# Moving the first weight slice, two early loads and two groups' attention steps in a fused attention and FFN kernel

## The chip, the cores and the metric

The kernel runs on one core of one Trainium2 chip. The metric is the device time of one execution in microseconds (us). Times are shown beside a profile of a single execution, whose span runs from the first to the last instruction on the core.

The names used below: PE is TensorE (matmuls), PEld its weight loads, ACT is ScalarE, DVE is VectorE, POOL is GpSimd. SP is SyncE, which here only issues DMAs; its queue is worked off in order, so an entry that waits holds back those behind it.

## The reference

Attention in chunks of 64 tokens, then an FFN with a squared ReLU over all tokens:

```python
# q, k, v: (8, 8, 576, 64) float32; w_in: (512, 2048); w_out: (2048, 512)
scores = scale * np.matmul(q_c, k_c.transpose(0, 1, 2, 4, 3))   # within each chunk of 64
attn = np.exp(scores - max) ; attn = attn / sum
out = np.matmul(attn, v_c)                                      # (B, H, S, D)
x = out.transpose(0, 2, 1, 3).reshape(B * S, H * D)             # 4608 tokens x 512
h = np.maximum(x @ w_in, 0.0)
y = h * h @ w_out                                               # 4608 x 512
```

## The kernel before

**Tiling.** The 4608 tokens are cut into 18 groups of 256 (GT), and the groups into nine blocks of two: block 0 is groups 0 and 1, block 1 is 3 and 2 (in that order), then 4 and 5, 6 and 7, and so on. So block 3 is groups 6 and 7. In each block PE does the FFN of its 512 tokens, and between these matmuls the attention of the next block's groups, so that PE always has FFN matmuls to do while other engines work on the attention.

**Steps of a group.** Loads of q, k and v (`qk_pieces`, `v_pieces`: lists of DMAs on SP; v goes in separate pieces of even and odd heads, L117 and L124). Transposed q and k, called qkT: groups 0 to 3 on PE (`transpose_qk`, L164 and L173; TE, TA and TM differ in the PSUM banks), the others by a cast to bf16 on POOL (C, `cast_qk`, L212) and a DMA transpose on SP (TD, L219). Scores (SC, `scores`, L233 on PE, then Exp on ACT, L240). Values (AV, `values`, L257 on PE, two tiles; then a reciprocal and a product on DVE, L264 and L265, which give x). Transposed x, called xT (XT): groups 0 and 1 on PE a tile at a time (`transpose_x_early`, L195, L200), groups 2 to 5 on PE (L284), from group 6 on by a DMA transpose on SP (L278). xT of both groups is the moving operand of the block's FFN-in.

**FFN.** FFN-in (`ffn_in`, L316) has 16 steps of four matmuls over the block's columns, one step for each 128 of the 2048 hidden features; each ends in a Relu on ACT (L322) and a square on DVE (L323). FFN-out (`ffn_out`, L332) has four row tiles of 16 matmuls each, with a yield after every fourth; the result is copied on ACT (L349) and stored by POOL (L350). Block 0 uses `ffn_out_by_ft` (L361), which takes the w_out slices in order of arrival: 12 yields over the hidden features for all four tiles, then four, one for each tile.

**What sets the order.** Nothing reorders the instructions of an engine. Each `yield` of the FFN ends a slot; at a slot the loop at the end issues one load from `loads` (if the slot is in `go_slots`) and then the steps that `at(slot, step, group)` put down for it. In blocks 2 and later slots 0 to 15 are FFN-in and 16 to 31 FFN-out. The loads run one or two blocks ahead.

**Buffers and queues.** Weights come as 16 slices of 512 KB in float32 (eight of w_in by `load_w_in`, eight of w_out by `load_w_out`) through five staging buffers (`w_st`), and are cast to bf16 on POOL (L139, L147). So the sixth slice waits on SP for the cast of the first, and so on. In addition SP's DMAs use eight completion semaphores in turn: an entry waits for the one eight before it. `keep_busy(n)` issues n matmuls of the identity whose result nobody reads.

**The start.** SP loads q, k, v of groups 0 and 1. PE works through their attention with `keep_busy` in between. The first slice of w_in is issued from ACT's queue, in two casts; the other seven follow on SP behind the values of group 1. The generator `early` does FFN-in of the first two hidden steps in two halves, first for the 256 columns of group 0, then for group 1; two of these half steps are run before the last transpose of x. Then come eight w_out slices, then the loads of group 3 and of group 2.

Of the kernel before, what the change touches and what calls it, by code (L numbers as in the profile page):

```python
# [17 lines left out]
def kernel(  # L18
# [9 lines left out]
    nc = tc.nc  # L28
# [8 lines left out]
    n_ft = d_ff // 128  # L37
# [3 lines left out]
    blocks = [[0, 1], [3, 2]] + [[g, g + 1] for g in range(4, n_grp, 2)]  # L41
# [87 lines left out]
    def go(pieces):  # L129
        for f in pieces:  # L130
            f()

    def load_w_in(i, eng=nc.sync, n_cast=1):
        cols = slice(i * 256, (i + 1) * 256)
        st = wst_pool.tile([128, 1024], FP32, name="w_st").rearrange("p (a f) -> p a f", a=n_dt)
        eng.dma_start(out=st, in_=moe_w_in[:, cols].rearrange("(a p) f -> p a f", p=128))
        n = 256 // n_cast
        for c in range(0, 256, n):
            nc.gpsimd.tensor_copy(  # L139
                out=w_in_bf[:, :, i * 256 + c:i * 256 + c + n], in_=st[:, :, c:c + n])  # L140

    def load_w_out(i):
        st = wst_pool.tile([128, 1024], FP32, name="w_st").rearrange("p (a f) -> p a f", a=2)
        nc.sync.dma_start(
            out=st,
            in_=moe_w_out[i * 256:(i + 1) * 256, :].rearrange("(a p) f -> p a f", p=128))
        nc.gpsimd.tensor_copy(out=w_out_bf[:, 2 * i:2 * i + 2, :], in_=st)  # L147
# [40 lines left out]
    def transpose_x_early(g, t):  # L188
        j, c = place[g]
        if j not in xTs:  # L190
            xTs[j] = att_pool.tile([128, BT // 128, n_dt, 128], BF16, name="xT", bufs=2)
        psb = ps_ffn.tile([128, 512], FP32, name="ps_ffn").bitcast(BF16)
        x = state["x", g]
        for hp in range(n_hp):
            nc.tensor.transpose(  # L195
                out=psb[:, hp * 128:(hp + 1) * 128],
                in_=x[:, t, hp].rearrange("p a d -> p (a d)"),
                identity=ident)
        copy = nc.vector.tensor_copy if t else nc.scalar.copy
        copy(  # L200
            out=xTs[j][:, c // 128 + t].rearrange("p h q -> p (h q)"), in_=psb[:, 0:512])

    def keep_busy(n):
        ps = ps_ffn.tile([128, 512], FP32, name="ps_ffn")
        for _ in range(n):
            nc.tensor.matmul(out=ps[:, 0:128], lhsT=ident, rhs=ident, start=True, stop=True)  # L206
# [84 lines left out]
    C, TD = cast_qk, transpose_qk_dma  # L291
    SC, AV, XT = scores, values, transpose_x
# [4 lines left out]
    def TE(g):  # L297
        transpose_qk(g, ps_ffn, ps_ffn)
# [10 lines left out]
    def ffn_in(j, parts):  # L309
        if j not in gTs:  # L310
            gTs[j] = ffn_pool.tile([128, n_ft, BT], BF16, name="gT")
        gT, xT = gTs[j], xTs[j]
        for c, n, ft in ((c, n, ft) for c, n, fts in parts for ft in fts):
            h = ps_ffn.tile([128, 512], FP32, name="ps_ffn")
            for dt in range(n_dt):
                nc.tensor.matmul(  # L316
                    out=h[:, 0:n],
                    lhsT=w_in_bf[:, dt, ft * 128:(ft + 1) * 128],
                    rhs=xT[:, c // 128:(c + n) // 128, dt, :],
                    start=(dt == 0), stop=(dt == n_dt - 1))  # L320
            rl = ffn_pool.tile([128, 512], BF16, name="rl", bufs=3)
            nc.scalar.activation(out=rl[:, 0:n], in_=h[:, 0:n], func=AF.Relu)  # L322
            nc.vector.tensor_tensor(  # L323
                out=gT[:, ft, c:c + n], in0=rl[:, 0:n], in1=rl[:, 0:n], op=ALU.mult)
            yield
# [28 lines left out]
    def ffn_out_by_ft(j):  # L354

        gT = gTs.pop(j)
        n_tt = len(blocks[j]) * GT // 128
        o_ps = [ps_ffn.tile([128, d_model], FP32, name="ps_ffn") for _ in range(n_tt)]

        def mm(tt, ft):  # L360
            nc.tensor.matmul(  # L361
                out=o_ps[tt],
                lhsT=gT[:, ft, tt * 128:(tt + 1) * 128],
                rhs=w_out_bf[:, ft, :],
                start=(ft == 0), stop=(ft == n_ft - 1))

        for ft in range(n_ft - 4):
            for tt in range(n_tt):
                mm(tt, ft)
            yield  # L370
        for tt in range(n_tt):
            for ft in range(n_ft - 4, n_ft):
                mm(tt, ft)
            o_sb = ffn_pool.tile([128, d_model], FP32, name="o_sb", bufs=4)
            nc.scalar.copy(out=o_sb, in_=o_ps[tt])
            t0 = blocks[j][tt // 2] * GT + tt % 2 * 128
            nc.gpsimd.dma_start(out=out[t0:t0 + 128, :], in_=o_sb)
            yield

    def pieces(grps):  # L380
        for g in grps:
            yield from qk_pieces(g)
        for g in grps:
            yield from v_pieces(g)

    go(pieces([0, 1]))
    TE(0)
    keep_busy(8)
    SC(0)
    keep_busy(6)  # L390
    TE(1)
    load_w_in(0, nc.scalar, 2)
    keep_busy(8)
    SC(1)
    keep_busy(10)
# [5 lines left out]
    keep_busy(10)  # L401
    transpose_x_early(0, 1)
    AV(1, [0])
    keep_busy(14)
    transpose_x_early(1, 0)
    keep_busy(8)
    AV(1, [1])
    n_early = 2
    early = ffn_in(0, [(0, 256, range(n_early)), (256, 256, range(n_early)),
                       (0, 512, range(n_early, n_ft))])  # L410
    next(early)
    next(early)
    transpose_x_early(1, 1)

    for i in range(1, 8):
        load_w_in(i)
    for i in range(8):
        load_w_out(i)
    for g in blocks[1]:
        go(pieces([g]))  # L420

    for j, grps in enumerate(blocks):
        nxt = blocks[j + 1] if j + 1 < len(blocks) else []
        far = blocks[j + 2] if j + 2 < len(blocks) else []
        plan = {}

        def at(slot, f, g):
            plan.setdefault(slot, []).append((f, g))

        if j == 0:  # L430
            loads, go_slots = pieces(far), range(17)
            for slot, f in ((24, TA), (27, SC), (29, AV), (31, XT)):
                at(slot, f, nxt[0])
            at(31, TM, nxt[1])
            phases = [early, ffn_out_by_ft(0)]
        elif j == 1:
            loads, go_slots = itertools.chain(*map(qk_pieces, far)), range(30, 48)
            for slot, f in ((3, SC), (6, AV), (11, XT)):
                at(slot, f, grps[1])
            for i, g in enumerate(nxt):  # L440
                for slot, f in ((16 + 4 * i, C), (21 + 4 * i, TD), (37, SC), (39 + 2 * i, AV),
                                (42 + 2 * i, XT)):
                    at(slot, f, g)
            for i, g in enumerate(far):
                at(36 + 4 * i, C, g)
                at(42 + 3 * i, TD, g)
            phases = [ffn_in(1, [(0, 256, range(n_ft)), (256, 256, range(n_ft))]), ffn_out(1)]
        else:
            loads, go_slots = pieces(far), range(32)
            slots = {SC: 9 if j == 3 else 8, AV: 11, XT: 15, C: 14, TD: 19}  # L450
            if j == 2:
                loads = itertools.chain(*map(v_pieces, nxt), loads)
                slots = {SC: 6, AV: 11, XT: 14, C: 20, TD: 24}
            for i, g in enumerate(nxt):
                at(slots[SC], SC, g)
                at(slots[AV] + 4 * i, AV, g)
                at(slots[XT] + 3 * i, XT, g)
            for i, g in enumerate(far):
                at(slots[C] + 2 * i, C, g)
                at(slots[TD] + 3 * i, TD, g)  # L460
            phases = [ffn_in(j, [(0, BT, range(n_ft))]), ffn_out(j)]
        slot = 0
        for phase in phases:
            for _ in phase:
                if slot in go_slots:
                    for f in loads:
                        f()
                        break
                for f, g in plan.get(slot, []):
                    f(g)  # L470
                slot += 1
        go(loads)
# [30 lines left out]
```

## Time and profile before

| | us |
|---|---|
| five runs | 301.45, 298.99, 296.71, 299.39, 298.08 |
| median | 298.99 |
| the profiled execution | 301.45 |
| its span | 299.7 |
| mean granted PE clock in it | 0.992 |
| FFN-in starts without a break (first L316 run) | 21.88 |
| FFN-out of block 0 starts (first L361) | 34.85 |
| block 2: FFN-in starts | 86.73 |
| block 2: FFN-out starts | 107.36 |
| block 3: FFN-in starts | 121.18 |
| last block: last L332 ends | 295.8 |

The profiled execution is the slowest of the five, so a sum over its parts is a sum against 301.45 and not against the median. From 121 us on each block takes 29.4 us (121.18, 150.71, 180.08, 209.44, 238.81 are the starts of FFN-in), and PE is busy almost throughout.

Where PE waits is read in its timeline from the bracket behind a row: idle time before the instruction, and what ended it. Where DMAs are late, the time to landing of a tile's DMAs says how long after its issue a transfer was complete. Some of them, issue and landing (us from the span's start):

| DMA | issued | landed |
|---|---|---|
| w_in, first slice (ACT's queue) | 12.09 | 18.55 |
| w_in, second slice (first one on SP) | 12.41 | 20.0 |
| w_out, last slice | 34.15 | 40.2 |
| k of group 3 | 35.08 | 43.85 |
| k of group 2, second part | 45.14 | 52.2 |
| qkT of group 5 | 71.41 | 75.63 |
| qkT of group 7 | 88.61 | 96.48 |
| xT of group 6 | 106.00 | 110.2 |
| qkT of group 9 | 121.00 | 127.7 |

### The profile page before, as it was taken

The page shows a single profiled execution, that of the slowest core. Times are in us where ns is not written, and L with a number is a line of the kernel's source. Part 1 is how long each engine was busy: PE and PEld are TensorE (multiplying, and loading weights), DVE is VectorE, ACT ScalarE, POOL GpSimd, SP SyncE. Part 2 cuts the span into 40 slices and gives each one's busy share as a digit, 9 for nine tenths or more (in the row PEclk, how much of TensorE's full clock was granted, in tenths as well). Part 3 has the DMA queues.
Part 4 walks back from the last instruction along what each step waited for, and adds up shares of the span by engine and source line. Part 5 has one row for each costly group of instructions (what it writes and reads, how often), then busy time and mean ns, then how long its engine had stood idle before and what let it go on. Part 6 is the DMA issues. An engine that isn't in the chain of part 4 may idle for free.

```text
span 299.7 us, 6440 instructions
## 1 busy us (share of the span) xinstructions
PE 282.2 (94%) x2608; PEld 142.8 (48%) x2628; DVE 114.4 (38%) x248; ACT 131.4 (44%) x228; POOL 67.6 (23%) x103
## 2 busy tenths in 40 slices
PE   2989999999895999999999999999999999999994
PEld 2764445885442444444444444444444444444441
DVE  1267812782422350355037405630562046205300
ACT  1526505773335531572167216711671177126511
POOL 2047832050070006023105013301320100020010
PEclk9999999999999799999999999999999999999999
DMA  7999999999999999998999899689987501310011
GB/s 206 240 346 364 331 290 218 292 198 209 209 219 175 227 195 230 241 220 170 254 243 222 168 267 248 112 165 276 241 133 152 161 35 24 83 72 35 0 70 70
DMA packets 156140, 57.03 MB, mean 190 GB/s; under 512 B 139280, under 2 KB 151824, under 8 KB 156112
## 3 DMA queue, kind: packets, MB, share of 16 engines
q1 hardware_dynamic: 152640, 46.81, 75.8%
q0 software_dynamic: 2800, 9.18, 9.2%
q10 hardware_dynamic: 672, 0.66, 0.7%
q8 instruction: 20, 0.33, 0.5%
q14 instruction: 8, 0.07, 0.1%
HBM read 36.70 MB, written 9.44 MB: 154 GB/s over the span
## 4 chain that ended last, share of the span: by engine, by line
PE 76%; DMA 17%; POOL 1%; issue 1%; DVE 1%; SPq 1%; ACT 1%; POOLq 0%; ACTq 0%
PE ps_ffn L316 34%; PE ps_ffn L332 33%; DMA k_sb<-in_k_dram 5%; DMA w_st<-in_moe_w_in_dram 4%; DMA qkT<-qkb 4%; PE ps_att L257 2%; PE ps_ffn L361 2%; DMA w_st<-in_moe_w_out_dram 2%; PE ps_att L233 2%; DMA q_sb<-in_q_dram 2%; DVE gT L323 1%; PE ps_ffn L164 1%; SPq L219 1%; POOL w_in_bf L139 1%; PE ps_ffn L206 1%
## 5 line engine op out<-in xcount | busy, mean ns | idle before, releaser
L316 PE MATMUL ps_ffn<-xT,w_in_bf 128*128 128x512 bf16 (+1 forms) x648 | 130.9, 359 | 1.3 <-DVE xT L200 1.1
L323 DVE TENSOR_TENSOR gT<-rl 128x512 bf16<-128x512 bf16 (+1 forms) x162 | 77.3, 493 | 131.8 <-ACT rl L322 129.7
L332 PE MATMUL ps_ffn<-w_out_bf,gT 128*128 128x512 bf16 x495 | 111.5, 379 | 1.1 <-issue 0.3
L322 ACT ACTIVATE rl<-ps_ffn 128x512 bf16<-128x512 f32 (+1 forms) x162 | 86.7, 553 | 39.8 <-PE ps_ffn L316 36.2
L316 PEld LDWEIGHTS <-w_in_bf 128*128 128x128 bf16 x648 | 62.3, 98 | 62.0 <-issue 2.8
L332 PEld LDWEIGHTS <-gT 128*128 128x128 bf16 x512 | 49.3, 98 | 58.0
L349 ACT COPY o_sb<-ps_ffn 128x512 f32<-128x512 f32 x31 | 18.2, 586 | 91.9 <-PE ps_ffn L332 91.9
L350 POOL DMA_DIRECT2D out_dram<-o_sb x31 | 16.8, 542 | 144.1 <-ACT o_sb L349 144.1
L212 POOL CAST qkb<-q_sb 128x1024 bf16<-128x1024 f32 x14 | 14.8, 1057 | 48.3 <-DMA q_sb<-in_q_dram 46.1
L265 DVE TENSOR_TENSOR x<-ps_att,rec 128x512 bf16<-128x512 f32 x36 | 24.9, 692 | 1.2
L240 ACT ACTIVATE e<-ps_att 128x1024 bf16<-128x1024 f32 x18 | 17.9, 1023 | 7.7 <-PE ps_att L233 7.7
L212 POOL CAST qkb<-k_sb 128x1024 bf16<-128x1024 f32 x14 | 15.4, 1098 | 2.1 <-DMA k_sb<-in_k_dram 2.0
L361 PE MATMUL ps_ffn<-w_out_bf,gT 128*128 128x512 bf16 x61 | 14.3, 379 | 0.3 <-issue 0.2
L264 DVE RECIPROCAL rec<-ps_att 128x8 f32<-128x8 f32 x36 | 7.2, 200 | 16.9 <-PE ps_att L257 16.9
L139 POOL CAST w_in_bf<-w_st 128x1024 bf16<-128x1024 f32 (+1 forms) x9 | 8.8, 981 | 19.1 <-DMA w_st<-in_moe_w_in_dram 19.1
L233 PE MATMUL ps_att<-qkT 64*64 64x64 bf16 x576 | 7.7, 197 | 4.6 <-DMA qkT<-qkb 4.2
L233 PEld LDWEIGHTS <-qkT 64*64 64x64 bf16 x576 | 6.0, 110 | 9.0 <-DMA qkT<-qkb 4.4
L257 PEld LDWEIGHTS <-e 64*64 64x64 bf16 x576 | 6.4, 107 | 7.0 <-DVE gT L323 2.5
L361 PEld LDWEIGHTS <-gT 128*128 128x128 bf16 x64 | 6.0, 98 | 7.2 <-issue 0.3
L147 POOL CAST w_out_bf<-w_st 128x1024 bf16<-128x1024 f32 x8 | 8.9, 1110 | 2.3 <-DMA w_st<-in_moe_w_out_dram 2.0
L257 PE MATMUL ps_att<-ve_sb,e 64*64 64x65 bf16 x288 | 8.6, 196 | 0.0
L257 PE MATMUL ps_att<-vo_sb,e 64*64 64x65 bf16 x288 | 8.6, 196 | 0.0
(34 smaller groups left out, 53.5 us busy)
## 6 DMA issues: line engine op xcount, KB each, us to landing
out_dram<-o_sb POOLq DMA_DIRECT2D x35, 256.0 KB, 4.1
q_sb<-in_q_dram SPq DMA_DIRECT2D x25, 256.0 KB, 5.2
k_sb<-in_k_dram SPq DMA_DIRECT2D x25, 256.0 KB, 4.9
ve_sb<-in_v_dram SPq DMA_DIRECT2D x32, 128.0 KB, 4.1
vo_sb<-in_v_dram SPq DMA_DIRECT2D x32, 128.0 KB, 3.9
w_st<-in_moe_w_out_dram SPq DMA_DIRECT2D x8, 512.0 KB, 5.8
w_st<-in_moe_w_in_dram SPq DMA_DIRECT2D x7, 512.0 KB, 7.1
q_sb<-in_q_dram SPq DMA_DIRECT2D x3, 512.0 KB, 6.7
```

Source lines behind the costliest of these rows:

```text
L212: nc.gpsimd.tensor_copy(out=qkb[:, which], in_=qk[g][which].rearrange("p t h d -> p (t h d)"))
L233: nc.tensor.matmul(out=ps[64 * c:64 * c + 64, o0:o0 + 64], lhsT=qkT[64 * a:64 * a + 64, 1, t, hp, cols], rhs=qkT[64 * a:64 * a + 64, 0, t, ...
L240: nc.scalar.activation(out=e.rearrange("p a h t q -> p (a h t q)"), in_=ps, func=AF.Exp, scale=scale)
L257: nc.tensor.matmul(out=ps[64 * p:64 * p + 64, a, hp * (D + 1):(hp + 1) * (D + 1)], lhsT=e[64 * c:64 * c + 64, a, hp, t, :], rhs=vb[64 * c: ...
L265: nc.vector.tensor_tensor(out=x[:, t].rearrange("p h a d -> p a h d"), in0=o[:, :, :, 0:D], in1=rec.to_broadcast([128, 2, n_hp, D]), op=AL ...
L316: nc.tensor.matmul(out=h[:, 0:n], lhsT=w_in_bf[:, dt, ft * 128:(ft + 1) * 128], rhs=xT[:, c // 128:(c + n) // 128, dt, :], start=(dt == 0) ...
L322: nc.scalar.activation(out=rl[:, 0:n], in_=h[:, 0:n], func=AF.Relu)
L323: nc.vector.tensor_tensor(out=gT[:, ft, c:c + n], in0=rl[:, 0:n], in1=rl[:, 0:n], op=ALU.mult)
L332: nc.tensor.matmul(out=o_ps, lhsT=gT[:, ft, tt * 128:(tt + 1) * 128], rhs=w_out_bf[:, ft, :], start=(ft == 0), stop=(ft == n_ft - 1))
L349: nc.scalar.copy(out=o_sb, in_=o_ps)
L350: nc.gpsimd.dma_start(out=out[t0:t0 + 128, :], in_=o_sb)
L361: nc.tensor.matmul(out=o_ps[tt], lhsT=gT[:, ft, tt * 128:(tt + 1) * 128], rhs=w_out_bf[:, ft, :], start=(ft == 0), stop=(ft == n_ft - 1))
```

## The change

Four things are changed. The arithmetic is the same.

1. The first w_in slice is issued from SP, directly behind the loads of groups 0 and 1, in place of ACT's queue between the transposes and the scores of group 1. It keeps its two casts.
2. `early` is gone: FFN-in of block 0 runs all 16 steps on 512 columns. The values of group 1's second tile stand before the transpose of its first tile, and 32 `keep_busy` matmuls instead of 22 stand between the values of group 1's first tile and FFN-in.
3. q and k of group 3 and the first piece of its values stand on SP before the sixth, seventh and eighth w_out slice; the rest of group 3's loads follows, then group 2's.
4. In block 2 the scores of groups 6 and 7 stand at slots 8 and 11 instead of both at slot 6, the values at 14 and 18 instead of 11 and 15, the DMA transposes of x at 19 and 22 instead of 14 and 17. The casts (C) and transposes (TD) of groups 8 and 9 keep their slots.

On SP the second of these x transposes (group 7) comes behind five entries that stood behind it before: three full pieces and two half pieces of values of groups 8 and 9.

```diff
-    def load_w_in(i, eng=nc.sync, n_cast=1):
+    def load_w_in(i, n_cast=1):
...
-        eng.dma_start(out=st, in_=moe_w_in[:, cols].rearrange("(a p) f -> p a f", p=128))
+        nc.sync.dma_start(out=st, in_=moe_w_in[:, cols].rearrange("(a p) f -> p a f", p=128))
...
     go(pieces([0, 1]))
+    load_w_in(0, n_cast=2)
     TE(0)
     keep_busy(8)
     SC(0)
     keep_busy(6)
     TE(1)
-    load_w_in(0, nc.scalar, 2)
     keep_busy(8)
...
     AV(1, [0])
-    keep_busy(14)
-    transpose_x_early(1, 0)
     keep_busy(8)
     AV(1, [1])
-    n_early = 2
-    early = ffn_in(0, [(0, 256, range(n_early)), (256, 256, range(n_early)),
-                       (0, 512, range(n_early, n_ft))])
-    next(early)
-    next(early)
+    transpose_x_early(1, 0)
+    keep_busy(14)
     transpose_x_early(1, 1)
+    keep_busy(10)
 
     for i in range(1, 8):
         load_w_in(i)
-    for i in range(8):
+    for i in range(5):
         load_w_out(i)
-    for g in blocks[1]:
-        go(pieces([g]))
+    third = pieces(blocks[1][0:1])
+    for i in range(5, 8):
+        next(third)()
+        load_w_out(i)
+    go(third)
+    go(pieces(blocks[1][1:2]))
...
-            phases = [early, ffn_out_by_ft(0)]
+            phases = [ffn_in(0, [(0, 512, range(n_ft))]), ffn_out_by_ft(0)]
...
             if j == 2:
                 loads = itertools.chain(*map(v_pieces, nxt), loads)
-                slots = {SC: 6, AV: 11, XT: 14, C: 20, TD: 24}
+                slots = {SC: 8, AV: 14, XT: 19, C: 20, TD: 24}
             for i, g in enumerate(nxt):
-                at(slots[SC], SC, g)
+                at(slots[SC] + (3 * i if j == 2 else 0), SC, g)
                 at(slots[AV] + 4 * i, AV, g)
                 at(slots[XT] + 3 * i, XT, g)
```

## The prediction

> **What bounds the kernel now.** I read the page's busy shares first, then the chain of waits in order of time, then PE's timeline around each stop, and last the SP queue and the landing times of the transfers that end the stops.
>
> ```profile
> PE 282.2 (94%) x2608; PEld 142.8 (48%) x2628; DVE 114.4 (38%) x248; ACT 131.4 (44%) x228; POOL 67.6 (23%) x103
> ...
> PEclk9999999999999799999999999999999999999999
> DMA  7999999999999999998999899689987501310011
> ```
>
> PE has nearly all of the span, so only PE's stops and the stretches in which its clock is low can be won. The DMA engines are at nine tenths or more through slice 18 (a slice is 7.5 us, so to 135 us) and seldom under eight until slice 30, so a transfer moved forward pushes others back. The one 7 in the clock row is slice 14 (97 to 105 us). PE's stops are these rows of its timeline (start, length, what, idle before it in brackets):
>
> ```profile
> 21.88 13.13 PE L316 MATMUL ps_ffn<-xT,w_in_bf 128*128 128x256 bf16 x64 [1.14 <-DVE xT L200]
> ...
> 43.89 0.64 PE L164 MATMUL ps_att<-ident,k_sb 128*64 128x128 bf16 x16 [0.34 <-DMA k_sb<-in_k_dram]
> ...
> 75.67 0.45 PE L233 MATMUL ps_att<-qkT 64*64 64x64 bf16 x32 [0.97 <-DMA qkT<-qkb]
> ...
> 96.53 0.45 PE L233 MATMUL ps_att<-qkT 64*64 64x64 bf16 x32 [3.22 <-DMA qkT<-qkb]
> 96.90 6.18 PE L316 MATMUL ps_ffn<-xT,w_in_bf 128*128 128x512 bf16 x20
> ...
> 121.18 8.80 PE L316 MATMUL ps_ffn<-xT,w_in_bf 128*128 128x512 bf16 x40
> ```
>
> Four stops, 5.67 us, all before 97 us; after 121 us only the end has another. The first, second and fourth stand where the change works. The fifth row is a cost of the fourth stop: 20 matmuls in 6.18 us, 0.31 each, against 8.80 / 40 = 0.22 in the sixth. The clock by half microseconds shows why:
>
> ```profile
> 96.50:97.00 0.50, 0.47 (x33) 0.43 (x34) 0.00 (x0) 0.00 (x0) 0.00 (x0) 1.00 0.55 120
> ...
> 99.50:100.00 0.50, 0.50 (x2) 0.15 (x1) 0.21 (x1) 0.00 (x0) 0.00 (x0) 0.50 0.96 213
> ```
>
> The third number from the right is the granted clock: after the 3.22 us stop it is 0.50 from 97.1 to 100.5 (the half microseconds between these two rows and after them), and 20 matmuls cost 6.18 - 20 x 0.22 = 1.8 us too much. Last the SP queue, where the transposes of block 2 stand:
>
> ```profile
> 88.61 7.87 DMA qkT<-qkb
> ...
> 103.73 1.14 SPq L110 DMA_DIRECT2D k_sb<-in_k_dram  x1
> 106.00 2.33 SPq L278 DMA_TRANSPOSE xT<-x  x1
> ...
> 111.12 1.43 SPq L278 DMA_TRANSPOSE xT<-x  x1
> DMA to landing us min/median/max: 4.8/4.8/4.8
> ```
>
> The first row (chain) is the qkT of group 7, landed at 96.48. The last is the landing time of the second xT transpose, group 7's, asked for its window alone: 111.12 + 4.8 = 115.9. PE wants it at 121.18, 5.3 us later.
>
> **Part 1, the start.** Removed: four half-wide FFN steps (16 matmuls of 256 columns, two runs around the last transpose of x). Added: ten keep_busy matmuls (0.07 us each, from 0.72 for ten) and two full FFN steps in their place. Values of group 1's second tile move forward to about 17.7. The x of that tile then comes from VectorE at 18.14 + 0.2 + 0.7 = 19.1; transpose, keep_busy and copy (0.4) end near 20.2 to 20.4. The copy ends at 21.8 in the trace, because two squares of 1.15 us together stand ahead of it. The first w_in slice: its issue takes 0.44 us on ACT at 12.09; on SP it comes at 12.41 behind the values of group 1, and the seven others follow a slot (0.4 us) later. The engines are full then, so its landing is set by bytes: values first, then 512 KB at 1.5 us, about 18 to 18.9 against 18.55. The two casts of 0.6 us end by 20.1, in time. FFN-in of block 0 is 64 matmuls of (34.85 - 21.88) / 60 = 0.216, so it ends at 20.3 + 13.8 = 34.1 instead of 34.85: gain 0.7. Bounds: 1.1 if it starts at the VectorE time, -0.5 if the slice lands 1.2 us late. Slices 1 to 7 have 0.9 us or more in hand.
>
> **Part 2, q and k of group 3.** The k now has two w_out slices less ahead of it (2 x 1.45 us): 43.85 - 2.9 = 41, before PE asks at 42.8. The stop of 0.34 goes. The last three w_out slices are delayed by q, k and one values piece. The last lands near 44.2 (was 40.2) and is cast by 45.3; PE needs it at about 46.9 (48.0 less the gains), so 1.6 us are left. SP is filled where it stood for a staging buffer: the DMA engines' share is 0.96 and 0.89 at 34 to 38 us, at 278 and 328 GB/s against some 350 before. That is (72 + 22) x 2 us / 350 = 0.5 us by which the whole stream behind moves up. The next thing late: k of group 2, issued 45.14, landing 7.1 us later at 52.24, when PE asks at 52.51. PE is 1.04 us earlier and stops for about 0.3.
>
> **What of that arrives.** Scores of group 5 wait until 75.63 for qkT. That transpose stands in SP's queue behind values of group 5 and hangs on the stream, not on PE. It moves up by 0.5 only, so of parts 1 and 2 only 0.5 us passes, and the stop grows from 0.97 to some 1.6.
>
> **Part 3, block 2.** A slot is four matmuls, 0.87 us. Scores of group 7 move from slot 6 to slot 11: 86.73 + 12 x 0.87 + 0.4 = 97.5, past the landing at 96.48 by 1.0; both move with the stream. So 3.22 us of stop go, and the 1.8 of half clock with them: 5.0, and PE would be at block 3 at 121.18 - 5.0 - 0.5 = 115.7. The values move to slots 14 and 18, the x transposes to 19 and 22. PE's work is the same. The two Exp of 1.02 us are three slots apart instead of together, on ACT with 0.27 free per slot and four ps_ffn banks in between; the reciprocals and products of the values (0.9 us a tile) run on VectorE, for group 7 now in FFN-out, where it has nothing else. On POOL nothing moves, but the output stores ahead of the casts of groups 8 and 9 come earlier, and these casts now hang on k of group 9 alone (about 111.5, cast by 113.7, before SP is at its transpose). All this costs nothing as long as xT of group 7 is there. On SP it moves behind q, k of group 9, three values pieces, the first transpose, two half pieces and a values piece. From the k row above (issued 103.73, landed 5.5 later at 109.2) I go on at the stream's own pace: q and k 1.3 each (six of them land from 102.8 to 109.2), values pieces of 128 KB 0.6, x transposes 1.4: 109.2 + 2.6 + 1.8 + 1.4 + 0.6 + 0.6 + 1.4 = 117.6, and about 0.6 for an output store (256 KB at the 350 to 400 GB/s of long rows) that now falls into the same stretch; less 0.5 for the stream: 117.7. PE waits from 115.7 to 117.7, 2.0 us: the cover of 5.3 us is used up. Bounds: 115 if it comes 3.3 after its issue at 111.8 (the median of its kind), which is no wait, and 119 if three stores fall in.
>
> Behind it, qkT of group 9 (issued 121.00, landed 127.7) loses the gap in which SP stood from 104.87 to 106.00 and comes at 126.2 or so; PE asks at 117.7 + 9.1 = 126.8. No stop, with 0.6 us in hand (1.0 of stop if that gap was worth nothing). Later blocks: xT at 146.7 for 150.7, qkT at 153.4 for 158.5: enough for 3.5 us.
>
> **The sum.** Block 3 begins at 117.7 instead of 121.18: 3.5 us. The profiled execution took 301.45 (span 299.7 and 1.75 around it): 298.0. It was the slowest of five; the median is 2.46 lower. What separates them enters: the Trainium skill (TensorE: Matmul & The Clock Gate, Why this matters for your kernels) wants no idle gap of PE over about 3 us, and its Part 1 says that the window which judges this runs freely and varies by run. The row shows the drop at 3.22 us, and none after 1.14 and 0.97. If the row holds in every execution, the change is worth 3.5 off the median: 295.5. By the rule a gap this near the limit drops the clock in some executions only. Without the drop, PE is at block 3 1.8 earlier before the change, and the gain is 3.5 - 1.8 = 1.7: 297.3. Since 1.8 of the 2.46 can be just this drop, which the changed kernel does not have, I carry only the rest: 298.0 - 0.7 = 297.3.
>
> **The rivals.**
> A, the forecast, 0.46: the wait for qkT of group 7 goes and a shorter one for xT of group 7 comes. 297.3, own range 295.5 to 298.8.
> B, 0.28: xT is in time. For it: the twelve x transposes land 3.0 to 4.8 us after issue, median 3.3; against: the 4.8 is the very one that counts. PE then has its full gain of 5.5: 301.45 - 5.5 - 0.7 = 295.2.
> C, 0.12: the DMA engines are the bound: three stores fall in ahead of xT and the stream does not move up, 117.6 + 1.8 = 119.4, with the clock held. Gain 1.8: 301.45 - 1.8 - 0.7 = 299.0.
> D, slower, 0.14: xT of group 7 lands so late that PE stands over 3 us at the head of block 3 and the half clock comes there. From a landing at 119.5 on (121.2 - 1.7) it decides: at 121.0 block 3 runs 1.5 us later than before, 301.45 + 1.5 = 303. For it: the full DMA row; against: the ten transfers from q of group 9 on would have to take 12 us instead of 8.
> That the change doesn't do what it says can be left out: the kernel writes out its own order, and PE's and SP's instructions stand as it says.
>
> **How the numbers follow.** About 1% is what a measurement of this kernel can tell from no change: 296.0 and 302.0. Under 296.0 lie three quarters of B and a quarter of A: 0.33. Over 302.0 lie most of D and little else: 0.11. The rest, 0.56, is within. The range reaches from B's better end (0.5 stream gain more, 294.0) to C with one late transpose more (1.4), 300.4.
>
> **What would show it.** Right: no stop before the scores of group 7, clock at 1.00 from 90 to 110 us, a stop of 1 to 3 us released by a DMA on xT at the first L316 of block 3, the stop at the scores of group 5 near 1.6, FFN-in of block 0 from about 20.3, no stop on k of group 3. Wrong: scores of group 7 still waiting, or L316 of block 3 beginning without a stop (B), or w_out slices waited for at the end of block 0.

## The result and the profile after

| | before | changed |
|---|---|---|
| median, us | 298.73 (75 runs) | 299.18 (38 runs) |
| ratio | | 1.0019, 95% interval 0.9999 to 1.0039 |
| profiled execution, us | 301.45 | 300.69 |
| its span, us | 299.7 | 298.9 |
| its mean granted PE clock | 0.992 | 0.994 |

No difference that can be measured, where I had forecast 1.7 us less than the median then shown. The page of the changed kernel, the three rows that were shown of before:

```profile
PE 282.1 (94%) x2610; PEld 141.9 (47%) x2630; DVE 115.2 (39%) x246; ACT 130.9 (44%) x226; POOL 68.1 (23%) x103
...
PEclk9999999999999999799999999999999999999999
DMA  7999999999999999999999699789887601310011
```

The 7 in the clock row has not gone. It has moved on by three slices, from 97 to 105 us to 119 to 127 us. PE's timeline shows what stands there:

```profile
22.49 12.26 PE L316 MATMUL ps_ffn<-xT,w_in_bf 128*128 128x512 bf16 x56 [1.19 <-POOL w_in_bf L139]
...
43.12 0.61 PE L164 MATMUL ps_att<-ident,k_sb 128*64 128x128 bf16 x16
...
52.98 0.64 PE L164 MATMUL ps_ffn<-ident,k_sb 128*64 128x128 bf16 x16 [0.90 <-DMA k_sb<-in_k_dram]
...
74.68 0.80 PE L233 MATMUL ps_att<-qkT 64*64 64x64 bf16 x64
...
97.02 0.45 PE L233 MATMUL ps_att<-qkT 64*64 64x64 bf16 x32
...
118.70 10.49 PE L316 MATMUL ps_ffn<-xT,w_in_bf 128*128 128x512 bf16 x40 [2.87 <-DMA xT<-x]
```

The four old stops are gone: FFN-in began at 19.41 without one, and k of group 3 (43.12), qkT of group 5 (74.68) and qkT of group 7 (97.02) have no idle time before them. Three new ones stand in their place: 1.19 us for the second w_in slice, 0.90 for k of group 2, and 2.87 us at the head of block 3 for xT. The last is followed by 40 matmuls in 10.49 us instead of 8.80. The windows of the changed kernel around it (the third number from the right is the granted clock):

```profile
118.50:119.00 0.50, 0.30 (x2) 0.18 (x3) 0.00 (x0) 0.00 (x0) 0.00 (x0) 1.00 1.37 220
119.00:119.50 0.50, 0.50 (x3) 0.15 (x2) 0.00 (x0) 0.00 (x0) 0.00 (x0) 0.66 1.30 250
119.50:120.00 0.50, 0.50 (x3) 0.17 (x2) 0.00 (x0) 0.00 (x0) 0.00 (x0) 0.50 1.28 291
...
122.50:123.00 0.50, 0.50 (x4) 0.22 (x3) 0.42 (x1) 0.02 (x1) 0.00 (x0) 0.93 0.09 9
```

It is the picture of before, 22 us later: a stop of some 3 us, then half clock for 3.4 us. PE ended block 2 at 115.83 (118.70 - 2.87) instead of 121.18, so 5.35 us had been won; 2.87 + 1.7 us of them are given back in the next 8 us. The 0.78 us that remain are the difference of the two profiled executions (301.45 and 300.69). The transpose that PE waited for, on SP's queue, and its time to landing:

```profile
112.72 1.32 SPq L278 DMA_TRANSPOSE xT<-x  x1
...
DMA to landing us min/median/max: 5.9/5.9/5.9
```

Most of what follows needs the granted clock of every run. One stretch of 3.4 us at half clock in 299 us takes the mean to 0.994, so I call runs under 0.9965 runs with half clock (no run of this case has a mean of 0.995 or 0.996). In the 38 timed runs of the changed kernel and its profiled one there are 17 of 39. The comparisons leave out executions that are over 1.5% above the fastest of their kernel, and these are mostly runs with half clock, so the ratios below say little of how often it comes and can differ from those of the medians, which are over all runs.

### The profile page after: what moved, and what is told of

The parts are those of the page before. It is cut to its first block, busy times and chain, and to the rows that moved or that the text cites. A ratio compares the mean times of both kernels' runs of the same rounds, so it can differ in the third digit from the quotient of the medians.

```text
span 298.9 us, 6440 instructions
## 1 busy us (share of the span) xinstructions
PE 282.1 (94%) x2610; PEld 141.9 (47%) x2630; DVE 115.2 (39%) x246; ACT 130.9 (44%) x226; POOL 68.1 (23%) x103
## 4 chain that ended last, share of the span: by engine, by line
PE 76%; DMA 11%; SPq 7%; DVE 2%; POOL 1%; issue 1%; ACT 1%; ACTq 0%
PE ps_ffn L316 36%; PE ps_ffn L332 36%; DMA w_st<-in_moe_w_in_dram 5%; DMA k_sb<-in_k_dram 2%; SPq L124 2%; SPq L102 2%; DMA w_st<-in_moe_w_out_dram 2%; DMA xT<-x 2%; PE ps_att L257 2%; PE ps_att L233 2%; SPq L117 2%; DVE gT L323 1%; SPq L136 1%; POOL w_in_bf L139 1%; DVE x L265 0%
## 5 line engine op out<-in xcount | busy, mean ns | idle before, releaser
L316 PE MATMUL ps_ffn<-xT,w_in_bf 128*128 128x512 bf16 (+1 forms) x640 | 130.8, 361 | 4.3 <-DMA xT<-x 2.9
L316 PEld LDWEIGHTS <-w_in_bf 128*128 128x128 bf16 x640 | 61.4, 98 | 65.8 <-DMA xT<-x 3.4
L361 PE MATMUL ps_ffn<-w_out_bf,gT 128*128 128x512 bf16 x61 | 14.3, 379 | 0.3 <-issue 0.2
```

What stands on the lines that cost most here:

```text
L316: nc.tensor.matmul(out=h[:, 0:n], lhsT=w_in_bf[:, dt, ft * 128:(ft + 1) * 128], rhs=xT[:, c // 128:(c + n) // 128, dt, :], start=(dt == 0) ...
L361: nc.tensor.matmul(out=o_ps[tt], lhsT=gT[:, ft, tt * 128:(tt + 1) * 128], rhs=w_out_bf[:, ft, :], start=(ft == 0), stop=(ft == n_ft - 1))
```

## The experiments

All times in us. "Half clock" is the share of such runs; the next column is the median of the runs without. The runs were taken in four series, each on another chip and with its own runs of before, so a row is compared with the before of its series. Over the four series before has 115 runs without half clock, median 297.75, and 104 with it, median 300.10 (one run of 373.41 us in series 1 is not counted here).

Two ways of counting the parts are in use. For a and b they are the four points of "The change". From h on, and in the text below, part 1 is the start (points 1 and 2), part 2 the early loads (point 3), as in the prediction. "Good slots" are those of c: scores at 8 and 11 as in the change, values at 12 and 16, x transposes at 14 and 17.

| series | kernel | median | half clock | without | ratio to before (95%) |
|---|---|---|---|---|---|
| 1 | before | 299.04 | 31 of 67 | 297.75 | |
| 1 | a: before, point 4 alone | 298.75 | 10 of 22 | 297.89 | 0.9987 (0.9958 to 1.0016) |
| 1 | b: changed, old slots in block 2 | 298.46 | 4 of 14 | 297.77 | 0.9998 (0.9966 to 1.0030) |
| 1 | c: changed, good slots | 297.04 | 4 of 22 | 296.54 | 0.9958 (0.9929 to 0.9987) |
| 1 | d: changed, first slice on ACT | 299.38 | 9 of 22 | 297.17 | 0.9952 (0.9915 to 0.9988) |
| 2 | before | 299.40 | 38 of 75 | 297.84 | |
| 2 | e: changed, PE kept busy at block 3 | 300.88 | 12 of 22 | 298.91 | 1.0060 (1.0028 to 1.0093) |
| 2 | f: changed, xT of 6 and 7 on PE | 297.13 | 0 of 22 | 297.13 | 0.9960 (0.9933 to 0.9987) |
| 2 | g: good slots and ACT | 297.43 | 2 of 22 | 297.12 | 0.9945 (0.9917 to 0.9973) |
| 2 | h: before, good slots | 299.54 | 11 of 22 | 298.16 | 1.0018 (0.9986 to 1.0051) |
| 3 | before | 299.16 | 20 of 43 | 297.84 | |
| 3 | i: before, xT of 6 and 7 on PE | 300.50 | 8 of 22 | 299.74 | 1.0057 (1.0028 to 1.0086) |
| 3 | j: f and ACT | 296.80 | 1 of 22 | 296.80 | 0.9947 (0.9923 to 0.9971) |
| 4 | before | 298.74 | 16 of 35 | 297.50 | |
| 4 | o: c again | 296.87 | 0 of 12 | 296.87 | 0.9922 (0.9886 to 0.9958) |
| 4 | p: h again | 296.31 | 3 of 12 | 296.07 | 0.9930 (0.9894 to 0.9967) |
| 4 | m: h and part 2 | 295.96 | 3 of 12 | 295.51 | 0.9952 (0.9907 to 0.9997) |
| 4 | n: h and part 1 | 298.02 | 4 of 12 | 297.28 | 0.9959 (0.9919 to 0.9998) |

### Which part gains, and which gives it back

a is before with the last hunk of the diff alone; b is the changed kernel without it:

```diff
-                slots = {SC: 6, AV: 11, XT: 14, C: 20, TD: 24}
+                slots = {SC: 8, AV: 14, XT: 19, C: 20, TD: 24}
...
-                at(slots[SC], SC, g)
+                at(slots[SC] + (3 * i if j == 2 else 0), SC, g)
```

> Before with part 4 of the change alone (scores at slots 8 and 11, values at 14 and 18, x transposes at 19 and 22 of block 2). Handed back (my theory): the stop before the scores of group 7 is gone, a stop of 2 to 4 us released by the DMA on xT stands at the first L316 of block 3, with or without half clock behind it; time within 1.5 us of before. Lost at the start (rival): part 4 gains its 3.2 to 5 us and only the start of the changed kernel eats them, so this kernel is 3 us or more faster than before, 295.5 or less.

> The changed kernel with the slots of block 2 as they were before (parts 1 to 3 alone). Handed back: the stop before the scores of group 7 is back with 2.5 to 4 us, no stop at the head of block 3; time 0 to 1 us below before, since only what the loads move up arrives. Lost at the start: 2 us or more slower than before, 301 or more.

In a's profile the head of block 3, in b's the scores of group 7:

```profile
117.39 8.81 PE L316 MATMUL ps_ffn<-xT,w_in_bf 128*128 128x512 bf16 x40 [1.32 <-DMA xT<-x]
```

```profile
93.62 0.45 PE L233 MATMUL ps_att<-qkT 64*64 64x64 bf16 x32 [1.16 <-DMA qkT<-qkb]
```

Both came as the theory of the gain handed back had it, except for the sizes. In a the stop at the scores of group 7 is gone, and 1.32 us stand at the head of block 3 (I had said 2 to 4). In b the stop at the scores is back, but with 1.16 us in place of 2.5 to 4. The start is not what eats the gain: a has the old start and is no faster than before.

### Where the transposes stand on SP

c keeps the scores at 8 and 11 and brings the values and x transposes forward, so that on SP both x transposes stand as in before: the first ahead of the last q and k of group 9, the second one values piece behind them. That of group 7 stands five entries earlier than in the changed kernel:

```diff
-                slots = {SC: 8, AV: 14, XT: 19, C: 20, TD: 24}
+                slots = {SC: 8, AV: 12, XT: 14, C: 20, TD: 24}
```

> The changed kernel with scores at 8 and 11, but values at 12 and 16 and the x transposes at 14 and 17 of block 2, so that both transposes stand on SP where they stood before. Handed back: no stop over 0.5 us at the scores of group 7 nor at the head of block 3, clock at 1.00 from 90 to 130 us, 295 to 296.5, that is 2.5 to 4 us less than before. Stream is the bound (rival): the stop only goes on to the scores of groups 8 and 9 in block 3, where qkT of group 9 lands at 126 or later, 1.5 to 3 us; 297.5 to 299. Lost at the start: no difference to the changed kernel, 299.

The x transposes on SP's timeline in c, and the first L316 of block 3 on PE's:

```profile
106.22 1.65 SPq L278 DMA_TRANSPOSE xT<-x  x1
110.56 2.24 SPq L278 DMA_TRANSPOSE xT<-x  x1
```

```profile
117.37 8.80 PE L316 MATMUL ps_ffn<-xT,w_in_bf 128*128 128x512 bf16 x40
```

The second was issued at 110.56 and landed 4.5 us later at 115.1, 2.3 us before PE wanted it; there is neither stop nor half clock. A stop of 0.59 us came instead at the scores of group 9 (qkT landed at 127.1), less than the rival's 1.5 to 3. The median is 2.0 below before, 297.04, half a microsecond over what I expected. So with the room at the scores and xT where it was, part of the gain stays.

f takes the two x transposes off the DMA queue altogether:

```diff
-    FIRST_DMA_X = 6
+    FIRST_DMA_X = 8
```

> The changed kernel with the x of groups 6 and 7 transposed on PE (16 matmuls more, 2 x 0.45 us) instead of by DMA, so nothing of xT stands on SP in block 2. Handed back: no stop at the head of block 3; cost 0.9 on PE and perhaps 0.3 of waiting for VectorE; runs without half clock near 297.5, few with it, median 297 to 298. Stream is the bound: the stop goes on to the scores of groups 8 and 9 (qkT lands at 122.5 or later, two transposes less ahead), median 298.5 to 299.5.

```profile
105.00 0.62 PE L284 MATMUL ps_att<-ident,x 128*128 128x128 bf16 x8
...
116.26 8.80 PE L316 MATMUL ps_ffn<-xT,w_in_bf 128*128 128x512 bf16 x40
124.99 0.74 PE L233 MATMUL ps_att<-qkT 64*64 64x64 bf16 x64
```

These rows of f's PE timeline show the added transposes, block 3 beginning at 116.26 with no stop, and the scores of groups 8 and 9 together and without one: their qkT landed at 119.5 and 122.3, against 123.6 and 125.5 in the changed kernel. None of 22 runs has half clock, and all lie between 296.3 and 299.5. That is 2.3 us under before in the medians and 0.7 among the runs without half clock (297.13 and 297.84); the added transposes take 0.62 us of PE a group. This is the clearest of the runs: most of what remained of the changed kernel's loss was the wait for xT.

i does the same to before, whose scores of group 7 stay at slot 6.

> Before with the x of groups 6 and 7 transposed on PE and nothing else changed (its slots of block 2 stay). If the change's part is to make room at the scores and the transposes on PE only keep that gain, this one still has the stop before the scores of group 7 (1 to 3.3 us) and half clock in a third or more of its runs: 298 to 299.5. If taking two transposes out of the DMA stream is all that matters (rival), it is as good as the changed kernel with them on PE: 297.1 with no half clock.

It is slower than before. Its profile has the stop at the scores of group 7 (1.66 us), block 3 begins at 117.89 against 115.92 in the second profile of before, and xT was not late in before, so PE pays for 16 transposes and gets nothing. The two edits need each other: room at the scores is lost to a late xT (a), and a timely xT is worth nothing without the room (i).

### Filling the stop

```diff
+        if j == 3:
+            keep_busy(24)
         slot = 0
```

> The changed kernel with 24 identity matmuls (1.35 us) put on PE between FFN-out of block 2 and FFN-in of block 3, where it stands idle for xT. If the half clock comes from this stop, shortening the idle to half of it takes most of the runs with a granted clock under 0.996 away (17 of 39 of the changed kernel): under 1 in 4, and the median falls by 0.5 to 1.2 us to 298.0 to 298.7, while the first L316 still begins within 1 us of the same time after the landing of xT. If the half clock comes from other stops (rival: the one at the scores of groups 4 and 5, or at group 2's transposes), its share stays at 0.4 and the time rises by up to 1 us where xT was in time.

A miss, and worse than the rival had it.

```profile
114.92 1.50 PE L206 MATMUL ps_ffn<-ident 128*128 128x128 bf16 x24
119.38 10.49 PE L316 MATMUL ps_ffn<-xT,w_in_bf 128*128 128x512 bf16 x40 [2.95 <-DMA xT<-x]
```

In this execution xT landed at 119.4, so that 2.95 us of idle remain behind the 24 matmuls and half clock follows all the same. The filler did not lower the share of half clock (12 of 22), and the runs without it have a median of 298.91, against 298.05 of the changed kernel in other runs. So 2.95 us behind dense work were enough for the drop here; whether a longer filler would hold the clock wasn't tried.

### Was the first profile of before an ordinary one

> The kernel before, one more profile. If the first profile was an ordinary one, the stop before the scores of group 7 is 2.8 to 3.6 us with half clock behind it. If it was one of the bad ones, the stop is 0.8 to 2 us and the clock 1.00.

> The changed kernel, one more profile. The stop at the head of block 3 is there again, 1 to 3 us, with half clock only if it is over 2.5; none at the scores of group 7.

The scores of group 7 in the second profile of before, and the head of block 3 in that of the changed kernel:

```profile
92.96 0.45 PE L233 MATMUL ps_att<-qkT 64*64 64x64 bf16 x32 [1.03 <-DMA qkT<-qkb]
```

```profile
119.38 8.81 PE L316 MATMUL ps_ffn<-xT,w_in_bf 128*128 128x512 bf16 x40 [1.75 <-DMA xT<-x]
```

k and l are the two kernels unchanged, and the profile of before that I had was not an ordinary one. With the scores at slot 6 the stop is 1.03 here (execution time 296.20), 1.16 in b, 1.66 in i, and 3.22 only in the profile that I predicted from. The stop for xT in the changed slots is 2.87, 1.32 (a), 2.95 (e), 1.75 (l) and none in d. The spread comes from when the DMA stream delivers: qkT of group 7 landed at 96.5 and 92.9 in the two profiles of before. Why it does so is not shown.

### The start

d, g and j issue the first slice from ACT as before (g with the slots of c, j with f's transposes on PE):

```diff
     go(pieces([0, 1]))
-    load_w_in(0, n_cast=2)
     TE(0)
...
     TE(1)
+    load_w_in(0, nc.scalar, 2)
     keep_busy(8)
```

> The changed kernel with the first w_in slice issued from ACT again, after the transposes of group 1. If the 1.95 us that the first weight issue takes on SP is what makes slice 2 late, slice 2 lands at about 20.0 instead of 21.1 and the stop of 1.19 us in the FFN-in of block 0 is under 0.3. Handed back: the time stays within 1 us of the changed kernel, since the head of block 3 waits for the transpose anyway, which moves up with the stream by at most 1 us. Lost at the start: 2 us or more less than the changed kernel, 297 or less.

> The changed kernel with both corrections: values at 12 and 16 and x transposes at 14 and 17, and the first w_in slice from ACT. Additive: 0.5 to 1 us below the version with the slots alone (297.0), 296.0 to 296.5. If the stream eats what the start gains: 297.0 again, with a longer stop at the scores of groups 5 or 9.

> The changed kernel with the x of groups 6 and 7 transposed on PE, and the first w_in slice from ACT. Start matters: 0.5 to 1 us below the version without the second correction (297.1), 296.1 to 296.6, no stop over 0.4 us in the FFN-in of block 0. Start is swallowed by the stop at the scores of groups 4 and 5: 297.1 again.

In d the second slice landed at 19.7 and the stop in the FFN-in of block 0 is gone, but the median is that of the changed kernel. g is 0.4 above c, j 0.3 below f, each in another series. The gains did not add up, and in the medians nothing here is larger than the spread between series. The first profile's 1.19 us was not ordinary either: in l the second slice came from SP at 19.4 and there was no stop.

The profiles say more. The cost of the first slice on SP shows at the loads of group 2, when block 0 ends. FFN-in of blocks 1 and 2 starts at (us):

| start of the kernel | profiles | block 1 | block 2 | stops at q and k of group 2 |
|---|---|---|---|---|
| as before | 6: before, k, a, h, i, p | 52.4 to 53.1 | 85.2 to 86.7 | none |
| parts 1 and 2 | 7: changed, l, b, c, e, f, o | 52.8 to 54.5 | 85.3 to 88.3 | 0.9 to 2.1 |
| part 2, first slice on ACT | 4: d, g, j, m | 52.0 to 52.6 | 84.9 to 85.9 | at most 0.34 |
| part 1 | 1: n | 55.9 | 89.4 | none (1.9 at group 3) |

d, g and j differ from the changed kernel, c and f in this one issue.

The last series asks whether parts 1 and 2 carry a gain that a late xT hides, since h, which is before with the slots of c, had come out 2.5 above c. o and p are c and h again; m adds to h the loads between the w_out slices (part 2), n the start alone (part 1: the first w_in slice on SP, and `early` gone).

> Before with only the slots of block 2 changed, and so that the x transposes keep their places: scores at 8 and 11, values at 12 and 16, x transposes at 14 and 17. Handed back: this alone gives the gain, 1 to 2.5 us below before, 296.5 to 298, about as good as the same slots in the changed kernel (297.0); few runs with half clock (under 1 in 4, against 31 of 67 before). Parts 1 and 2 matter (rival): it stays over 298.3.

> The changed kernel with values at 12 and 16 and x transposes at 14 and 17 once more: 296.5 to 297.8, half clock in under 1 run of 4. If the difference to the same slots in before was one of calls and chips: 298 to 299, within 0.7 of the other three.

> Before with these slots once more. If parts 1 and 2 carry a gain that the good slots uncover: 299 to 300 and half clock in 4 of 10 runs or more, stops at the scores of groups 8 and 9. If only block 2's slots decide: within 0.7 of the changed kernel with them, 297 to 297.8.

> Before with these slots and part 2 alone (q and k of group 3 between the last w_out slices). If the stream that moves up by half a microsecond is what makes room at the scores of groups 8 and 9: 297 to 298, most of the way to both parts. If part 1 is what counts: 299 to 300 as without both.

> The changed kernel with these slots, but the loads of group 3 behind all eight w_out slices as before (part 1 alone). If part 2 is what counts: 299 to 300. If part 1 counts: 297 to 298.

In one series the good slots give 296.31 with neither part, 295.96 with part 2, 296.87 with both and 298.02 with part 1 alone; p and m came out lower than I had expected. h's 299.54 did not come back. Its profile had stops of 1.41 and 2.20 us at the scores of groups 8 and 9 with half clock from 126.4 to 133.2, where p's has one of 1.22. Even without half clock the same kernel stands at 298.16 in one series and 296.07 in the other, and why is open. In this series parts 1 and 2 carry no hidden gain. Part 1 seems to cost (1.7 without part 2, 0.9 with it), and n shows how. PE's timeline:

```profile
43.34 0.64 PE L164 MATMUL ps_att<-ident,q_sb 128*64 128x128 bf16 x16 [0.80 <-DMA q_sb<-in_q_dram]
45.09 1.07 PE L164 MATMUL ps_att<-ident,k_sb 128*64 128x128 bf16 x16 [1.11 <-DMA k_sb<-in_k_dram]
```

With all eight w_in slices on SP and the loads of group 3 behind the last w_out slice, q and k of group 3 land at 43.3 and 45.1 (42.0 and 43.9 in the first profile of before), and two stops of 1.9 us together stand where before has 0.34; half clock follows, a mean of 0.52 in 45 to 47.5 us. Part 2 removes just these. With 12 runs each, differences under about 1 us between the four are not settled.

## Why the prediction was wrong

In short: the waits went and came where I had said, but the stop that goes is a third to a half as long in the other profiles as in the one that I had read, the stop that comes can halve the clock as well, and the start brings nothing to block 2. Step by step, with the profile of the changed kernel first.

**Start**: FFN-in began at 19.41, earlier than my 20.3, but waited 1.19 us at its third step. What failed is that the landings are set by bytes: in 12.5 to 15 us the engines moved 177 GB/s and in 17.5 to 20 us 258 (before: 229 and 355). The first weight issue on SP took 1.95 us, in before too (1.97), where the first slice had already left by ACT. So slice 2 was issued at 14.3 instead of 12.4 and landed at 21.1 instead of 20.0. Gain 0.27 at FFN-out for 0.7 forecast. That stop was of this execution: in six of the eight profiles with the first slice on SP slice 2 landed at 19.2 to 19.6.

**q and k of group 3**: right. k landed at 42.0 (41 forecast), its stop went, and the last w_out slice at 45.4 made nobody wait. k of group 2 was late by 0.90 instead of 0.3. This term stayed too small: in the seven profiles with parts 1 and 2 the stops at q and k of group 2 take 0.9 to 2.1 us.

**What arrives**: the stream moved up by 0.6 us at qkT of group 5 (0.5 forecast). The stop there did not grow to 1.6 (my own terms give 1.2: 0.97, plus 0.74 of lead behind the stop of 0.3, less 0.5) but vanished, since PE had spent its lead in the two stops above. The sum at block 2, 0.64, is near the 0.5 that I had, but by luck: over the profiles block 2 starts at a median of 86.1 with parts 1 and 2 and of 86.0 with the start of before.

**Block 2**: the mechanism is rival and forecast in one. No stop at the scores, and PE at the end of the block at 115.83 for 115.7 forecast. xT of group 7 was issued at 112.7 (111.8) and landed 5.9 us later at 118.7, not 117.7. This term, the 2.0 us of "PE waits from 115.7 to 117.7", was 2.87 in that execution, and it brought 1.7 us of half clock, which I had put only into rival D from an idle of over 3 us on. The Trainium skill (TensorE: Matmul & The Clock Gate, Why this matters for your kernels) sets the limit at about 3 us; here 2.87 was enough, and 1.75 and 1.41 in one execution (l) were not. I had put the half clock behind this stop at nothing because it was to stay under 3 us; the last section shows from which share of idle time it came here. So the forecast's 117.7 with full clock became 118.7 with half.

**From the profile to the median**: here the sum fell. I took the 3.22 us of the profiled execution as the stop that goes, and 1.8 of half clock as a cost of before that the changed kernel would not have. In the other profiles the stop that goes is 1.0 to 1.7 us, the one that comes is 1.3 to 2.9 (none in d), and half clock is as frequent in both (104 of 219 runs and 17 of 39). The runs without it have medians of 297.75 and 298.05 in different series: nothing gained where I had 1.7. My sum for these, 3.22 + 0.5 - 2.0, becomes 1.0 to 1.7, plus nothing, less 1.3 to 2.9. The gain in block 2 was paid back at the head of block 3, in the executions with half clock and in those without. f, which takes away only that payment, is at 297.13 and never at half clock.

The version that beats before is that with c's slots: 297.0 and 296.9 with the rest of the change, against 299.0 and 298.7 of before in the same series, and once 296.0 with part 2 alone, against 298.7. With neither part they gave 299.5 once and 296.3 once. With xT of groups 6 and 7 on PE instead (f and j) the changed kernel is as good.

Open: what makes the stream early or late by 3.6 us from one execution of before to the next, and which stops bring half clock in half of its runs; one of its two profiles has it, behind the stop of 3.22, and the other has none.

## What to carry to other kernels

When a DMA queue is full, a step that moves its consumer later makes room only for what is fetched; what the step itself sends through the queue moves later with it, so count the entries that it falls behind and compare with the time at which the faster engine will ask. Before a stop in a profile is taken as the gain, see whether the execution is an ordinary one of its kernel: the median of the runs and the mean clock of each tell, and here the profile lay 2.5 us over the median, with a stop that was a third as long in the next profile. A gain that also shortens the time to the next wait should be followed to the second wait, with the clock.

## What the runs showed of the hardware

**The clock.** The granted clock fell to half for 3.41 us behind stops of 3.22, 2.87 and 2.95 us and stayed at 1.00 behind single stops of 1.75, 1.66 and 1.63. Two shorter stops close together brought it as well: 0.80 and 1.11 in n, and 1.41 and 2.20 in h, where the drop came 0.4 us into the second. So the length of the longest stop doesn't decide. What fits every profile is a fixed grid. In each of the 18 the clock changes only at times that lie whole multiples of 3.413 us apart (in before at 97.12, 100.53 and 298.50: one step and 58), and where the grid lies differs from execution to execution. If an execution is cut into these stretches, half clock follows each stretch in which PE was busy for less than half: 0.59 us of 3.41 in before, 0.54 in the changed kernel, 0.46 in e, 1.51 in n, 1.60 and 1.61 in h, and under 1.1 at the end of every profile, when PE has run out of work. In the 1477 other stretches of the 18 profiles, from the first at full clock on, PE was busy for 1.73 us or more, and full clock followed each. Stretches of h (the first number behind the comma is PE's busy time) and of l, whose stop of 1.75 us the grid cuts at 119.25:

```profile
122.99:126.40 3.41, 1.60 (x38) 0.64 (x36) 1.28 (x3) 1.60 (x4) 0.00 (x0) 1.00 1.21 209
126.40:129.81 3.41, 1.61 (x35) 0.94 (x36) 0.00 (x0) 1.60 (x2) 0.00 (x0) 0.50 1.03 228
129.81:133.23 3.42, 3.42 (x39) 1.26 (x38) 0.62 (x2) 1.30 (x3) 1.04 (x1) 0.50 1.25 207
```

```profile
115.84:119.25 3.41, 1.79 (x9) 0.59 (x7) 0.00 (x0) 0.59 (x1) 0.54 (x1) 1.00 1.16 238
119.25:122.67 3.42, 3.29 (x16) 1.52 (x17) 0.85 (x2) 1.68 (x3) 0.00 (x0) 1.00 1.24 300
```

By these figures (an estimate) a single stop must put some 1.7 us or more into one stretch. One of 1.0 us can't bring half clock alone, one of 2.0 does if most of it falls into one stretch, and even 2.87 can be cut into two of 1.43 that don't. That can be why the same kernel has half clock in some executions only; without a profile of each it is not shown.

Half clock shows in a run's mean clock as 0.994 or less, so its frequency can be counted without a profile: about half of the runs of this kernel had it, and the changed kernel with 16 small transposes moved to PE had it in none of 22.

**The queue.** In each of the 18 profiles one issue on SP between 11.8 and 12.6 us took 1.4 to 2.0 us, where the two right behind it took 0.5 to 0.7. Mostly it is the first weight slice (1.95 in the changed kernel, 1.97 in before and in n), but in d and g it is the values piece before it (1.57 and 1.68). So it is not the size of the load that holds the queue there; what does is open.
